# GpSimd's SBUF passes tied to VectorE's 16-bit passes, and other planned times, in a one-core attention block

## The chip, the cores and the metric

The kernel runs on one core of a Trainium2 chip. The metric is the device time of one execution in microseconds; three runs of the kernel before have a median of 369.49 us (368.03 to 369.72).

## The reference

One attention block on x of 1 x 2048 x 448 in bf16, with 16 heads of 28 columns:

```python
qkv = (x @ wqkv).reshape(B, S, 3, H, Dh).transpose(2, 0, 3, 1, 4)
q, k, v = qkv[0], qkv[1], qkv[2]
scores = einsum("bhqd,bhkd->bhqk", q, k) * Dh ** -0.5
p = softmax(scores, axis=-1)
o = einsum("bhqk,bhkd->bhqd", p, v)
return o.transpose(0, 2, 1, 3).reshape(B, S, D) @ wo
```

## The kernel before

The sixteen heads are four groups g of four, and the 2048 queries four chunks c of 512. A set s is one (g, c); there are sixteen, in the order `ORDER`. Each head of a set has sixteen key tiles of 128, so a set is 64 steps of a 128 x 512 block of scores. The heads sit in strips of 32 partitions, 28 of them used; the rows left over carry a bound of the scores, so that the exponentials need no maximum of the row, and a column of ones in V gives the denominators.

A step's exponentials are made in one of two ways. On ScalarE, one activation (line 891, `pt<-a`) takes two steps at once out of a two-bank PSUM tile `a0` or `a1`. On VectorE, a pass over PSUM (line 906, `I<-d`) turns scores into the 16 bits of a bf16 power of two, and two further passes over SBUF (line 929, `J<-I`, 16 bits to 16 bits, up to four steps at once) make shifted copies of them; three weighted copies of V (`VT`, scaled at line 552) bring the three terms together in TensorE's sum `o` (line 987).

The order of the instructions on every engine is written at build time by a planner: a loop at the end of the function keeps a clock for each of TensorE, ScalarE, VectorE, SyncE and GpSimd, takes the engine whose clock is lowest, lets its `pick_` function choose an operation that is ready, and emits it. An operation (`Op`) has a planned duration, the events that it needs and gives, a `lag` that is added to the time at which it is ready, and a `land` that is added to its end before others may use its result (for DMAs). How many steps go each way falls out of this. On the chip the engines run their queues in the emitted order and wait on semaphores for data alone; the planned times are not seen there.

Operations that the planner keeps apart have `port=True`: such an operation of VectorE starts no earlier than the planned end of GpSimd's last one, and the other way round, by the two times in `port`. A J pass reads and sets the same times in `do_add` and `pick_dve`. On GpSimd these are the squares (`square`, line 297, `sq<-KA` and `sq<-QA`), which the norms of keys and queries are summed from, and the products (`mul`, line 1038, `xs<-o_sb,rr` and `OTL<-o_sb,rr`), which divide a set's output. On VectorE they are the J passes, the scaled copies of V, the passes that make `su` and `kmt`, and the reciprocal (line 1025).

When a set is complete, `finish_set` queues this chain: VectorE copies `o` to `o_sb` (line 1016); SyncE's DMA gathers the denominators to `den` (line 1021); VectorE makes the reciprocal `rec`; DMAs write it to `scr` in DRAM (line 1030) and spread it to all rows as `rr` (line 1035); GpSimd multiplies. The output projections (`oproj_job`, and `early_jobs` for the last chunk) need the products of all four groups of a chunk. SyncE's one queue also carries the rows of Q (line 441), the bounds `su` (line 506) and the stores of the output (line 573).

Of the kernel before, what the change touches and what calls it, by code (L numbers as in the profile page):

```python
# [8 lines left out]
ALU = mybir.AluOpType  # L9
AX = mybir.AxisListType  # L10
BF16 = mybir.dt.bfloat16
F32 = mybir.dt.float32
I16 = mybir.dt.int16
# [24 lines left out]
def kernel(  # L38
# [7 lines left out]
    nc = tc.nc  # L46
# [239 lines left out]
    def quarters(out, lhsT, rhs, start, stop, **k):  # L286
        for i in range(P // HP):
            r = slice(HP * i, HP * (i + 1))
            nc.tensor.matmul(out=out[r, :], lhsT=lhsT[:, r], rhs=rhs, start=start, stop=stop, tile_position=(0, HP * i), **k)  # L289

    def new_sq(key):
        sqt[key] = wk.tile([P, QW], BF16, name="sq", tag="sq", bufs=4)
        return sqt[key]

    def square(key, src):
        t = new_sq(key)
        nc.gpsimd.tensor_tensor(out=t[:], in0=src, in1=src, op=ALU.mult)  # L297

    def act_square(key, mask):
        t = new_sq(key)  # L300
# [2 lines left out]
    def k_job(g, sc, bank, pri, gate=0, split=2):  # L303
        key = ("K", g, sc)
        n = CC // split

        def mm(part):
            if part == 0:
                held[key] = bank_tile(bank) if bank[0] != "a" else pair_tile(bank)
            mm_proj(held[key][:, 0:QW], 1, g, sc, range(part * n, (part + 1) * n))  # L310

        def evac():
            KAt[(g, sc)] = big.tile([P, QW], BF16, name=f"KA{sc}", tag=f"KA{sc}", bufs=2)
            src = held[key][:, 0:QW]
            nc.vector.tensor_scalar(out=KAt[(g, sc)][:], in0=src, scalar1=kmask[:, 0:1],  # L315
                                    scalar2=ones[:, 0:1], op0=ALU.mult, op1=ALU.add)

        for p in range(split):
            add("PE", n * D_WAVE, lambda p=p: mm(p), pri=pri, gate=gate, cols=448 * n,
                need=[("XT", sc, 0), ("XT", sc, 1), ("W", 1)] + ([key + (p - 1,)] if p else []), gives=[key + (p,)],  # L320
                acq=bank if p == 0 else None)
        add("DVE", 0.72, evac, need=[key + (split - 1,)], gives=[key], rel=bank, pri=pri)
        add("POOL", 1.15, lambda: square(key, KAt[(g, sc)][:]), need=[key], gives=[("ksq", g, sc)], pri=pri, port=True)

    def kn_job(g, bank, pri, gate=0):
        key = ("KN", g)

        def mm(sc):
            if sc == 0:
                held[key] = bank_tile(bank) if bank[0] != "a" else pair_tile(bank)  # L330
            quarters(held[key][:, 0:QW], maskK[:, sc, :], sqt.pop(("K", g, sc))[:], sc == 0, sc == NQC - 1)

        def red():
            kst[g] = wk.tile([P, 1], F32, name="kst")
            nc.vector.reduce_max(out=kst[g][:], in_=held.pop(key)[:, 0:QW], axis=AX.X)

        def spread_rows():
            a = wk.tile([P, HP], F32, name="kbc")
            nc.vector.tensor_copy(out=a[:], in_=kst[g][:].to_broadcast([P, HP]))
            b = wk.tile([P, HP], F32, name="kbt")  # L340
            nc.vector.transpose(out=b[:], in_=a[:])
            kmt[g] = wk.tile([P, 1], F32, name="kmt")
            nc.vector.reduce_max(out=kmt[g][:], in_=b[:], axis=AX.X)

        for sc in range(NQC):
            add("PE", D_WAVE, lambda sc=sc: mm(sc), pri=pri, gate=gate, cols=512,
                need=[("ksq", g, sc)] + ([("KNp", g, sc - 1)] if sc else []), gives=[("KNp", g, sc)],
                acq=bank if sc == 0 else None)
        add("DVE", 0.61, red, need=[("KNp", g, NQC - 1)], gives=[("kst", g)], rel=bank, pri=pri)
        add("DVE", 0.65, spread_rows, need=[("kst", g)], gives=[("km", g)], pri=pri, port=True)  # L350
# [66 lines left out]
    def q_job(g, c, bank, pri, gate=0, split=2):  # L417
        key = ("Q", g, c)
        n = CC // split
        first = (g, c) == (0, 0)  # L420

        def mm(part):
            if part == 0:
                held[key] = bank_tile(bank) if bank[0] != "a" else pair_tile(bank)
            mm_proj(held[key][:, 0:QW], 0, g, c, range(part * n, (part + 1) * n))

        def evac():
            if first:
                t = qtt[0] = wk.tile([P, QW], BF16, name="qt0", bufs=1)
            else:  # L430
                t = QAt[(g, c)] = big.tile([P, QW], BF16, name=f"QA{c}", tag=f"QA{c}", bufs=1)
            if first:
                nc.vector.tensor_scalar(out=t[:], in0=held[key][:, 0:QW], scalar1=qmask[:, 0:1],
                                        scalar2=qoff[:, 0:1], op0=ALU.mult, op1=ALU.add)
            else:
                nc.vector.tensor_copy(out=t[:], in_=held[key][:, 0:QW])  # L436

        def rows():
            for i in range(HG):
                r = slice(HP * i, HP * i + Dh)  # L440
                nc.sync.dma_start(out=QP[c][i % 2][g % 2][r, :], in_=QAt[(g, c)][r, :])

        for p in range(split):
            add("PE", n * D_WAVE, lambda p=p: mm(p), pri=pri, gate=gate, cols=448 * n,
                need=[("XT", c, 0), ("XT", c, 1), ("W" if g else "G", 0)] + ([key + (p - 1,)] if p else []), gives=[key + (p,)],
                acq=bank if p == 0 else None)
        add("DVE", 0.72 if first else 0.61, evac, need=[("qsq", g, c) if first else key + (split - 1,)], gives=[key], rel=(bank, 2) if first else bank,
            pri=pri)
        if first:
            add("ACT", 0.62, lambda: act_square(key, qmask), need=[key + (split - 1,)], gives=[("qsq", g, c)],  # L450
                rel=(bank, 2), pri=pri)
        else:
            add("POOL", 1.15, lambda: square(key, QAt[(g, c)][:]), need=[key], gives=[("qsq", g, c)], pri=pri, port=True)
            add("SP", 2.4, rows, need=[key, ("QZ", c, g % 2)] + ([("Oset", ORDER.index((g - 2, c)))] if g > 1 else []),
                gives=[("QR", g, c)], land=1.6, pri=1)

# [28 lines left out]
    def qn_job(g, cs, bank, pri, gate=0):  # L485
# [7 lines left out]
        def bound():  # L493
            z = wk.tile([P, QW], BF16, name="z", bufs=1)
            nc.vector.tensor_scalar(out=z[:], in0=held.pop(key)[:], scalar1=kmt[g][:, 0:1], scalar2=MARG4 if g else 1.0,  # L495
                                    op0=ALU.mult, op1=ALU.mult)
            held[("su",) + key] = su = wk.tile([P, QW], BF16, name="su", bufs=1)
            nc.vector.tensor_scalar(out=su[:].bitcast(I16), in0=z[:].bitcast(I16), scalar1=0.5, scalar2=HALFE,
                                    op0=ALU.mult, op1=ALU.add)

        def place():
# [47 lines left out]
    def vs_job(g, b, pri):  # L549
        def scale(k):  # L550
            flat = (lambda v: v.rearrange("p t g e -> p (t g e)")) if g is None else (lambda v: v.rearrange("p t e -> p (t e)"))
            nc.vector.tensor_scalar(out=flat(VT[k][g, b]), in0=flat(VT[0][g, b]), scalar1=WT[k], scalar2=None, op0=ALU.mult)  # L552

        gs = [g] if g is not None else list(range(GH, G))
        for k in range(1, NTERM):
            add("DVE", 0.335 if g is None else 0.2, lambda k=k: scale(k), need=[("V", gs[0], XB * b + u) for u in range(XB)],
                gives=[("VS", gg, b, k) for gg in gs], pri=pri + 0.1 * k, port=True)
# [367 lines left out]
    def do_add(t):  # L925
        ch, m, k = adds[0]
        w = slice(0, m * QW)
        r = ch[k] = wk.tile([P, HG * QW], I16, name=f"J{k}", bufs=NCH)
        nc.vector.tensor_scalar(out=r[:, w], in0=ch["I"][:, w], scalar1=float(SHIFT[k]), scalar2=None, op0=ALU.add)  # L929
        end = port["DVE"] = t + m * QW * 0.00026 + 0.068  # L930
        for n in range(m):
            pending.append({"step": ch["steps"][n], "k": k, "ap": r[:, n * QW:(n + 1) * QW].bitcast(BF16),
# [71 lines left out]
    def finish_set(s, end):  # L1004
# [7 lines left out]
        st = {}  # L1012
# [9 lines left out]

        def recip():
            st["rec"] = wk.tile([P, HG * QW // P], F32, name="rec")
            nc.vector.reciprocal(out=st["rec"][:], in_=st["den"][:])

        def scatter():
            n = P // HG
# [6 lines left out]
            nc.sync.dma_start(out=st["rr"][:], in_=scr[:].unsqueeze(1).to_broadcast([HG, HP, QW]))  # L1035

        def mul():
            nc.gpsimd.tensor_tensor(out=otile(g, c), in0=st["o_sb"][:], in1=st["rr"][:], op=ALU.mult)  # L1038

        add("DVE", 0.61, evac, need=[("Oset", s)], gives=[("osb", s)], rel="o", pri=-5)  # L1040
        add("SP", 0.6, gather, need=[("osb", s)], gives=[("den", s)], land=1.5, pri=2)
        add("DVE", 0.16, recip, need=[("den", s)], gives=[("rec", s)], pri=50, port=True)
        add("SP", 0.35, scatter, need=[("rec", s)], gives=[("scr", s)], land=1.1, pri=2)
        add("SP", 0.5, spread, need=[("scr", s)], gives=[("rr", s)], land=5.5, pri=2)
        add("POOL", 1.4, mul, need=[("rr", s)], gives=[("OT", g, c)], pri=60, port=True)

    def best(eng, t):
        b, nxt = None, None
# [228 lines left out]
```

## Time and profile before

| what | value |
|---|---|
| three runs, median | 369.49 us |
| profiled execution | 368.69 us, span 366.9 us |
| granted clock of TensorE | 1.000 |
| busy: TensorE, VectorE, ScalarE, GpSimd | 345.5, 347.6, 348.9, 70.8 us |
| activations, line 891 | 366 |
| I passes, line 906; J passes, line 929 | 292; 146 |
| squares, line 297; products, line 1038 (GpSimd) | 27; 15 |

The busy times are of the profiled execution. A row of a group has the line, engine, operation, tiles out<-in, shapes and count, then busy time in us and mean ns of one, then the engine's idle time ahead of them with what ended most of it. A row of a timeline has the start and duration in us, the instruction, a count where several are merged, and in brackets the idle time before it with its releaser. A row by tile has the shortest, median and longest duration in ns.

### The profile page before, as it was taken

The page shows a single profiled execution, that of the slowest core. Times are in us where ns is not written, and L with a number is a line of the kernel's source. Part 1 is how long each engine was busy: PE and PEld are TensorE (multiplying, and loading weights), DVE is VectorE, ACT ScalarE, POOL GpSimd, SP SyncE. Part 2 cuts the span into 40 slices and gives each one's busy share as a digit, 9 for nine tenths or more (in the row PEclk, how much of TensorE's full clock was granted, in tenths as well). Part 3 has the DMA queues.
Part 4 walks back from the last instruction along what each step waited for, and adds up shares of the span by engine and source line. Part 5 has one row for each costly group of instructions (what it writes and reads, how often), then busy time and mean ns, then how long its engine had stood idle before and what let it go on. Part 6 is the DMA issues. An engine that isn't in the chain of part 4 may idle for free.

```text
span 366.9 us, 10993 instructions
## 1 busy us (share of the span) xinstructions
PE 345.5 (94%) x4528; PEld 112.3 (31%) x4529; DVE 347.6 (95%) x646; ACT 348.9 (95%) x381; POOL 70.8 (19%) x103
## 2 busy tenths in 40 slices
PE   8999999999999999999889999989988999999985
PEld 4433233422233333232222222222222222222223
DVE  7799999999899999899999999999999999999983
ACT  4689999999999999999999999999999999999992
POOL 8952122123010413121010413201010101010010
PEclk9999999999999999999999999999999999999999
DMA  8510100011000000010000001100000001010101
GB/s 256 123 42 15 28 29 7 4 35 36 18 31 28 6 6 30 15 42 28 15 19 3 30 3 55 31 21 12 19 14 9 26 29 54 19 65 27 46 14 50
DMA packets 15050, 12.30 MB, mean 34 GB/s; under 512 B 6808, under 2 KB 13080, under 8 KB 15000
## 3 DMA queue, kind: packets, MB, share of 16 engines
q1 hardware_dynamic: 13448, 10.18, 9.7%
q10 hardware_dynamic: 1040, 1.02, 0.9%
q8 instruction: 35, 0.57, 0.7%
q0 software_dynamic: 512, 0.40, 0.5%
q14 instruction: 15, 0.12, 0.1%
HBM read 7.58 MB, written 1.96 MB: 26 GB/s over the span
## 4 chain that ended last, share of the span: by engine, by line
PE 34%; ACT 30%; DVE 27%; issue 7%; DMA 1%; DVEq 0%; ACTq 0%
ACT pt L891 30%; DVE I L906 12%; PE a L699 12%; PE o L987 9%; DVE J L929 7%; PE m L289 4%; PE m L282 4%; DVE QP L180 1%; DVE V L540 1%; DVE QA L436 1%; DVE KA L315 1%; DVE z L495 1%; PE d L699 1%; DVE o_sb L1016 1%; DVE V L552 1%
## 5 line engine op out<-in xcount | busy, mean ns | idle before, releaser
L891 ACT ACTIVATE pt<-a 128x1024 bf16<-128x1024 f32 x366 | 337.6, 1145 | 3.0 <-PE a L699 1.4
L906 DVE TENSOR_SCALAR I<-d 128x512 int16<-128x512 f32 x263 | 170.7, 680 | 3.8 <-PE d L699 3.4
L699 PE MATMUL a<-QP,KA 32*128 32x512 bf16 (+1 forms) x720 | 141.0, 381 | 12.2 <-ACT pt L891 11.2
L987 PE MATMUL o<-pt,V 128*32 128x512 bf16 x732 | 104.2, 384 | 0.0
L929 DVE TENSOR_SCALAR J<-I 128x2048 int16<-128x2048 int16 x146 | 101.8, 724 | 0.3
L699 PEld LDWEIGHTS <-KA 32*128 32x128 bf16 (+1 forms) x1041 | 48.7, 91 | 151.2 <-issue 148.3
L699 PE MATMUL d<-QP,KA 32*128 32x512 bf16 (+1 forms) x258 | 83.3, 383 | 1.3 <-DVE I L906 1.3
L987 PE MATMUL o<-J,V 128*32 128x512 bf16 x584 | 76.6, 384 | 0.4 <-DVE J L929 0.3
L987 PE MATMUL o<-I,V 128*32 128x512 bf16 x292 | 68.6, 384 | 0.7 <-DVE o_sb L1016 0.5
L987 PEld LDWEIGHTS <-V 128*32 128x32 bf16 x1608 | 28.6, 94 | 49.6 <-issue 47.0
L1038 POOL TENSOR_TENSOR xs<-o_sb,rr 128x512 bf16<-128x512 f32 x12 | 16.4, 1370 | 105.9 <-DMA rr<-scr 65.0
L282 PE MATMUL m<-XT,WRAW 112*32 112x512 bf16 x384 | 29.6, 384 | 0.2 <-DVE V L540 0.2
L297 POOL TENSOR_TENSOR sq<-KA 128x512 bf16<-128x512 bf16 x12 | 12.5, 1041 | 69.6 <-DVE KA L315 69.6
L297 POOL TENSOR_TENSOR sq<-QA 128x512 bf16<-128x512 bf16 x15 | 16.4, 1091 | 47.4 <-DVE QA L436 47.4
L906 DVE TENSOR_SCALAR I<-m 128x512 int16<-128x512 f32 x29 | 19.7, 680 | 0.4 <-PE m L699 0.4
L289 PE MATMUL m<-WRAW,XT 112*32 112x112 bf16 (+1 forms) x768 | 18.1, 230 | 0.2 <-DVE V L540 0.2
L1038 POOL TENSOR_TENSOR OTL<-o_sb,rr 128x512 bf16<-128x512 f32 x3 | 4.2, 1403 | 56.0 <-DMA rr<-scr 36.7
L289 PEld LDWEIGHTS <-XT 112*32 112x32 bf16 x768 | 11.7, 96 | 10.3 <-issue 10.1
L289 PE MATMUL m<-WO,xs 128*32 128x448 bf16 x156 | 12.5, 359 | 0.0
L436 DVE CAST QA<-m 128x512 bf16<-128x512 f32 x15 | 10.2, 683 | 1.1 <-PE m L282 0.5
L699 PE MATMUL m<-QP,KA 32*128 32x512 bf16 x29 | 11.1, 384 | 0.0
L289 PE MATMUL m<-sq,maskK 128*32 128x512 bf16 x108 | 10.8, 388 | 0.1
(113 smaller groups left out, 192.0 us busy)
## 6 DMA issues: line engine op xcount, KB each, us to landing
rr<-scr SPq DMA_DIRECT2D x15, 256.0 KB
QP<-QA SPq DMA_DIRECT2D x60, 28.0 KB
out_dram<-osb SPq DMA_DIRECT2D x12, 112.0 KB
WRAW<-in_wqkv_dram SPq DMA_DIRECT2D x3, 392.0 KB
xs<-in_x_dram ACTq DMA_DIRECT2D x4, 224.0 KB
xs<-in_x_dram SPq DMA_DIRECT2D x4, 224.0 KB
QP<-su SPq DMA_DIRECT2D x32, 2.0 KB
out_dram<-pt SPq DMA_DIRECT2D x2, 224.0 KB
```

The lines of the kernel that those rows point to most:

```text
L180: nc.vector.memset(QP[c][k][z][:], 0.0)
L282: nc.tensor.matmul(out=ps[HP * i:HP * (i + 1), :], lhsT=w[:, cc, h * Dh:h * Dh + HP], rhs=XT[c][cc // 2][:, cc % 2, :], start=(cc == 0), s ...
L289: nc.tensor.matmul(out=out[r, :], lhsT=lhsT[:, r], rhs=rhs, start=start, stop=stop, tile_position=(0, HP * i), **k)
L297: nc.gpsimd.tensor_tensor(out=t[:], in0=src, in1=src, op=ALU.mult)
L315: nc.vector.tensor_scalar(out=KAt[(g, sc)][:], in0=src, scalar1=kmask[:, 0:1], scalar2=ones[:, 0:1], op0=ALU.mult, op1=ALU.add)
L436: nc.vector.tensor_copy(out=t[:], in_=held[key][:, 0:QW])
L699: nc.tensor.matmul(out=out_ap, lhsT=KAt[(g, j // XB)][r, (j % XB) * P:(j % XB + 1) * P], rhs=q[r, :], start=(n == 0), stop=(n == len(terms ...
L891: nc.scalar.activation(out=pt[:], in_=ps[:], func=ACT.Exp, scale=LN2 / 128.0)
L906: nc.vector.tensor_scalar(out=dst, in0=pd[:], scalar1=BIAS, scalar2=0.0, op0=ALU.add, op1=ALU.max)
L929: nc.vector.tensor_scalar(out=r[:, w], in0=ch["I"][:, w], scalar1=float(SHIFT[k]), scalar2=None, op0=ALU.add)
L987: nc.tensor.matmul(out=o[HP * i:HP * (i + 1), :], lhsT=VT[e["k"]][g, j // XB][:, j % XB, HP * i:HP * (i + 1)], rhs=e["ap"], start=(SETMM[k ...
L1038: nc.gpsimd.tensor_tensor(out=otile(g, c), in0=st["o_sb"][:], in1=st["rr"][:], op=ALU.mult)
```

## The change

`after_shared` gives an instruction a wait on the last VectorE instruction of certain kinds that the planner emitted ahead of it, kept in `cur["shared"]`. The squares of `square` and the products get this wait. Recorded in `cur["shared"]` are the J passes, the scaled copies of V, the pass that makes `su`, the last reduction of `kmt` and the reciprocal. The planned duration of these squares goes from 1.15 to 1.08 and of the products from 1.4 to 1.3; the reciprocal gets a lag of 2.0; the spread of `rr` lands after 7.0 instead of 5.5.

```diff
+    def after_shared(m):
+        if "shared" in cur:
+            tc.add_manual_dep(m.ins, cur["shared"].ins.name,
+                              mybir.DependencyInfo(mybir.DependencyClass.Sync, mybir.DependencyReason.DATA),
+                              reason="GpSimd's pass stays behind VectorE's")
...
     def square(key, src):
         t = new_sq(key)
-        nc.gpsimd.tensor_tensor(out=t[:], in0=src, in1=src, op=ALU.mult)
+        after_shared(nc.gpsimd.tensor_tensor(out=t[:], in0=src, in1=src, op=ALU.mult))
...
-        add("POOL", 1.15, lambda: square(key, KAt[(g, sc)][:]), need=[key], gives=[("ksq", g, sc)], pri=pri, port=True)
+        add("POOL", 1.08, lambda: square(key, KAt[(g, sc)][:]), need=[key], gives=[("ksq", g, sc)], pri=pri, port=True)
...
-            nc.vector.reduce_max(out=kmt[g][:], in_=b[:], axis=AX.X)
+            cur["shared"] = nc.vector.reduce_max(out=kmt[g][:], in_=b[:], axis=AX.X)
...
-            add("POOL", 1.15, lambda: square(key, QAt[(g, c)][:]), need=[key], gives=[("qsq", g, c)], pri=pri, port=True)
+            add("POOL", 1.08, lambda: square(key, QAt[(g, c)][:]), need=[key], gives=[("qsq", g, c)], pri=pri, port=True)
...
-            nc.vector.tensor_scalar(out=su[:].bitcast(I16), in0=z[:].bitcast(I16), scalar1=0.5, scalar2=HALFE,
+            cur["shared"] = nc.vector.tensor_scalar(out=su[:].bitcast(I16), in0=z[:].bitcast(I16), scalar1=0.5, scalar2=HALFE,
...
-            nc.vector.tensor_scalar(out=flat(VT[k][g, b]), in0=flat(VT[0][g, b]), scalar1=WT[k], scalar2=None, op0=ALU.mult)
+            cur["shared"] = nc.vector.tensor_scalar(out=flat(VT[k][g, b]), in0=flat(VT[0][g, b]), scalar1=WT[k], scalar2=None, op0=ALU.mult)
...
-        nc.vector.tensor_scalar(out=r[:, w], in0=ch["I"][:, w], scalar1=float(SHIFT[k]), scalar2=None, op0=ALU.add)
+        cur["shared"] = nc.vector.tensor_scalar(out=r[:, w], in0=ch["I"][:, w], scalar1=float(SHIFT[k]), scalar2=None, op0=ALU.add)
...
-            nc.vector.reciprocal(out=st["rec"][:], in_=st["den"][:])
+            cur["shared"] = nc.vector.reciprocal(out=st["rec"][:], in_=st["den"][:])
...
-            nc.gpsimd.tensor_tensor(out=otile(g, c), in0=st["o_sb"][:], in1=st["rr"][:], op=ALU.mult)
+            m = nc.gpsimd.tensor_tensor(out=otile(g, c), in0=st["o_sb"][:], in1=st["rr"][:], op=ALU.mult)
+            after_shared(m)
...
-        add("DVE", 0.16, recip, need=[("den", s)], gives=[("rec", s)], pri=50, port=True)
+        add("DVE", 0.16, recip, need=[("den", s)], gives=[("rec", s)], pri=50, lag=2.0, port=True)
...
-        add("SP", 0.5, spread, need=[("scr", s)], gives=[("rr", s)], land=5.5, pri=2)
-        add("POOL", 1.4, mul, need=[("rr", s)], gives=[("OT", g, c)], pri=60, port=True)
+        add("SP", 0.5, spread, need=[("scr", s)], gives=[("rr", s)], land=7.0, pri=2)
+        add("POOL", 1.3, mul, need=[("rr", s)], gives=[("OT", g, c)], pri=60, port=True)
```

## The prediction

> **What bounds the kernel now.** I read the page's busy times and costliest groups first, then ScalarE's waits and timeline, then GpSimd's and VectorE's timelines around the same moments.
>
> ```profile
> PE 345.5 (94%) x4528; PEld 112.3 (31%) x4529; DVE 347.6 (95%) x646; ACT 348.9 (95%) x381; POOL 70.8 (19%) x103
> ...
> L891 ACT ACTIVATE pt<-a 128x1024 bf16<-128x1024 f32 x366 | 337.6, 1145 | 3.0 <-PE a L699 1.4
> L906 DVE TENSOR_SCALAR I<-d 128x512 int16<-128x512 f32 x263 | 170.7, 680 | 3.8 <-PE d L699 3.4
> L929 DVE TENSOR_SCALAR J<-I 128x2048 int16<-128x2048 int16 x146 | 101.8, 724 | 0.3
> ```
>
> Three engines are full; GpSimd is idle four fifths of the span. The number of exponentials on ScalarE is fixed by the plan made at build time, so I take ScalarE as the ruler. From its start times in the trace: 366 activations begin at 18.86 us and the last ends at 358.97, 340.1 us; the median distance between two starts is 0.904 us; 366 x 0.904 = 330.9. So 9.1 us are lost between them, 1.0 of it before 26 us, where GpSimd has no pass yet. No removal of waits can give more than about 8 us unless the plan gives ScalarE fewer activations. The timeline of ScalarE has the visible part:
>
> ```profile
> 24.30 73.49 ACT L891 ACTIVATE pt<-a 128x1024 bf16<-128x1024 f32 x80 [0.25 <-PE d L699]
> 98.34 12.50 ACT L891 ACTIVATE pt<-a 128x1024 bf16<-128x1024 f32 x13 [0.55 <-PE a L699]
> 111.05 168.81 ACT L891 ACTIVATE pt<-a 128x1024 bf16<-128x1024 f32 x183 [0.21 <-PE d L699]
> 280.10 73.75 ACT L891 ACTIVATE pt<-a 128x1024 bf16<-128x1024 f32 x80 [0.24 <-PE m L699]
> 354.24 4.72 ACT L891 ACTIVATE pt<-a 128x1024 bf16<-128x1024 f32 x5 [0.40 <-PE a L699]
> ```
>
> The bracket is ScalarE's idle time and who ended it: always TensorE, coming late with scores. What made TensorE late stands in GpSimd's and VectorE's timelines (start, duration, idle before it), and in J's row by tile:
>
> ```profile
> 205.13 1.27 POOL L1038 TENSOR_TENSOR xs<-o_sb,rr 128x512 bf16<-128x512 f32 x1
> ...
> 205.19 1.76 DVE L929 TENSOR_SCALAR J<-I 128x2048 int16<-128x2048 int16 x1
> ...
> 350.18 1.28 POOL L1038 TENSOR_TENSOR xs<-o_sb,rr 128x512 bf16<-128x512 f32 x1 [20.03 <-DMA rr<-scr]
> ...
> 350.38 1.63 DVE L929 TENSOR_SCALAR J<-I 128x2048 int16<-128x2048 int16 x1
> ...
> L929 DVE TENSOR_SCALAR J<-I x146: 627/684/1766, 23.8 to 355.5; 128x2048 int16<-128x2048 int16 x146
> ...
> 96.20 0.25 DVE L1025 RECIPROCAL rec<-den 128x16 f32<-128x16 f32 x1 [1.09 <-DMA den<-o_sb]
> ```
>
> A J pass (median 684 ns) that begins just after a GpSimd pass ends 0.55 us after that pass: it stood still until GpSimd was done. Eight J of the 146 last over 1.1 us, all beside a GpSimd pass, at 39, 54, 107, 205, 231, 250, 288 and 350 us; together 6.1 us over the median. The last line is another loss: VectorE stood 1.09 us at a reciprocal whose denominators had not landed.
>
> **The change, part by part.**
>
> *Wait on VectorE's last shared pass.* The plan never lets a J and a GpSimd pass overlap, but nothing holds GpSimd to it. From the end of a reciprocal the old costs put the product 0.2+0.35+1.1+0.03+0.5+5.5+0.2 = 7.9 us later (8.0 from its start); in nine of fifteen sets it starts 6.5 to 7.2 us after the reciprocal's start. So it comes about a microsecond before its place and lands on a J planned ahead of it: 205, 250, 288, 350. At 39 a square slips between two J that the plan has back to back. The wait stops these. ScalarE's loss behind each, as the distances of its starts over 0.904: 0.26 (39), 0.49 (205), 0.24 (250), 0.39 (288), 0.52 (350), 1.90 in all. At 107 the loss is 0.37 + 0.13 = 0.50, but that product is late (10.2 us after its reciprocal, since the scatter waited in SP's queue behind the su copies), where only the third part below helps; I count half, 0.25. At 54 and 231 the square starts first, right behind its own evacuation, with the J behind it; the wait leaves these as they are: 0.
>
> What the wait costs: behind the waiting instruction on GpSimd stand only the next squares and products. Squares are read by TensorE's norm matmuls; the closest is the square that ends at 90.97 with its matmul at 91.76, 0.79 us of cover, more than one J (0.68). If the cover is gone, TensorE, in order, stands by the rest. Products are needed by the output projections many microseconds later. One more semaphore instruction on GpSimd is 17 ns, on an engine that is 19% busy: 0.
>
> *Squares planned at 1.08 instead of 1.15, products at 1.3 instead of 1.4.* Undisturbed they take 1.04 and 1.27 (the medians by tile). But now the pass starts behind a semaphore: a square behind its evacuation starts 0.14 us after it (QA ends at 80.67, the square starts at 80.81). So the pass ends 0.14 + 1.04 = 1.18 us after the J, where the plan lets the next J go at 1.08: 0.10 late. 21 of the 42 passes end within 0.35 us of the start of a J, so up to 2.1 us of VectorE. In the six collisions above ScalarE lost 2.40 us for 5.02 us of VectorE, 0.48 each: 0 to 1.0 us, and I take 0.5. The shorter costs also free 27 x 0.07 + 15 x 0.1 = 3.4 us of planned exclusion; an activation moved to VectorE costs it two I (2 x 0.6) and half a four-step share of two J (0.6), so at most two activations fewer, 1.8 us. The trace can't show a plan; nearest to zero, since VectorE found I passes to do beside most GpSimd passes. I take 0 and keep -1.8 for the range.
>
> *Reciprocal with a lag of 2.0.* It covers the 1.09 us at 96.2. ScalarE's loss there is one distance of 1.842 instead of 0.904: 0.94 gained. The other fourteen reciprocals had no wait and lose nothing, since nothing on the path waits for them. With the reciprocal its scatter and spread move (issue 0.33 and 0.55 us each on SP): they pass no more than they did, the Q rows and su copies stay in place ahead or behind, and those are needed only a set later.
>
> *Spread with 7.0 instead of 5.5.* The product's place is now 9.5 us from the reciprocal's start, 3.5 later from the gather; thirteen of the fifteen start within 9.5 now. It matters at the end: the product of the last set but one, at 350.18 now, comes at about 353 to 357, beside the last four J, and three early output-projection pieces of 0.19 us each move behind it. TensorE has the 0.24 us before 362.1 free and little else: 0 to 0.6, I take 0.2.
>
> Sum: -1.90 - 0.25 - 0.94 + 0.5 + 0.2 = -2.4 us. The profiled execution took 368.69 us (span 366.9 and 1.8 around it), so 366.3 for such a one; it lies 0.8 below the median of the three runs, 369.49, and the median goes to 367.1.
>
> **The rivals.** *Passes that come late (slower).* The wait holds GpSimd behind VectorE, but nothing holds the next J behind GpSimd. A pass that waits for a late J, or for a landing beyond the new cost (10.2 and 11.1 us occur), runs into the J planned after it, which then stands for up to 1.1 us. For: the 0.10 us handover above, the 21 passes with a J at their end, the SP queue. Against: the spare 1.5 us of the new costs. Price by the collisions above: 0.40 us of ScalarE for each blocked J. With the reciprocal's 0.94 gained, it decides from 11 blocked J instead of 8, and is slower by over 0.5% from 15 of 42; at 17, 9 x 0.40 - 0.94 = +2.7: 372.2 us.
> The Trainium skill (SBUF — State Buffer, section "Who interferes with whom") speaks for this rival: whichever of the two issues first has the shared port pair for its whole instruction, and the other blocks fully. By it a late pass costs a J as before, wait or no wait; the trace agrees at 205.19, where the J ends 0.55 us after GpSimd's pass.
>
> *Nothing measurable.* ScalarE's 8 us stay because most lie elsewhere: 278.66 (0.54), 238.79 (0.29), 102.9 and 104.1 (0.51 together) have no blocked J near them. If the collisions only fill time that would be lost anyway, the reciprocal's 0.94 less the 0.7 of costs remains: 369.2.
>
> *The plan deals better.* Every later decision follows the changed times; with two activations fewer and the stalls gone, -2.4 - 1.8 = -4.2: 365.3. The same dealing can give one or two more, which is in the range above.
>
> That the change doesn't do what it says is hardly possible for the wait; for the costs, a product that starts right behind a J would show it.
>
> **How the numbers follow.** Forecast 0.52, late passes 0.22, better deal 0.14, nothing 0.12. About 0.5% (1.85 us) is what a measurement of this kernel can tell from no change. Of the forecast, with its costs between 0 and 1.6 (a gain of 1.5 to 3.1), four fifths lie beyond that: 0.41 faster, 0.11 same. Faster 0.41 + 0.14 = 0.55; same 0.11 + 0.12 = 0.23; slower 0.22. The forecast's own range is 366.4 to 368.0; for 8 in 10 I go to 364.8 (past the better deal) and to 371.2, which leaves out half of the late passes.
>
> **What would show it.** Right: no J over 1.1 us except behind a square right after its evacuation; J near 690 ns on average; no VectorE wait for den; ScalarE's idle before L891 at 1.5 us or less with 365 to 367 activations; products starting 0.1 to 0.2 us behind a J. Wrong: as many long J as now, behind GpSimd passes that began later; an activation count off by two or more; TensorE waiting for sq; output pieces after 360 us.

## The result and the profile after

The changed kernel takes 366.32 us (median of 6 runs, 366.26 to 366.70) where the kernel before, timed in the same rounds too, has 369.21: 2.89 us less by the medians. The ratio, 0.9927 (95% interval 0.9912 to 0.9942), makes it 2.7 us. The forecast was 2.4 us less than before, 367.1 from a base of 369.49. The profiled execution has a span of 364.6 us against 366.9.

Line numbers are up by 7 or 8 in the changed kernel: activations stand at 898, I at 913, J at 936, the reciprocal at 1032, squares at 304, products at 1045. The page's busy times and groups, with the rows that answer to those shown before:

```profile
PE 346.3 (95%) x4515; PEld 115.5 (32%) x4515; DVE 343.8 (94%) x646; ACT 347.7 (95%) x381; POOL 68.0 (19%) x103
...
L898 ACT ACTIVATE pt<-a 128x1024 bf16<-128x1024 f32 x366 | 336.4, 1186 | 1.7 <-PE d L706 0.8
L913 DVE TENSOR_SCALAR I<-d 128x512 int16<-128x512 f32 x264 | 173.4, 683 | 7.3 <-PE d L706 6.5
L936 DVE TENSOR_SCALAR J<-I 128x2048 int16<-128x2048 int16 x146 | 98.5, 699 | 0.3
```

366 activations, 292 I and 146 J, as before: the plan gave no engine less to do. J costs 98.5 instead of 101.8 us, and VectorE now stands idle ahead of I for 7.3 us instead of 3.8: part of what it saved it only waits away. ScalarE's timeline shows where the time came from:

```profile
24.42 253.65 ACT L898 ACTIVATE pt<-a 128x1024 bf16<-128x1024 f32 x276 [0.25 <-PE d L706]
278.31 78.05 ACT L898 ACTIVATE pt<-a 128x1024 bf16<-128x1024 f32 x85 [0.24 <-PE d L706]
```

The visible holes at 98 (0.55), 111 (0.21) and 354 us (0.40) are gone; the one of 280 stays, now at 278. Counted by start times, what its 366 activations lose over 0.904 us each goes from 9.11 to 6.25 us. J by tile:

```profile
L936 DVE TENSOR_SCALAR J<-I x146: 630/686/1401, 23.9 to 354.0; 128x2048 int16<-128x2048 int16 x146
```

VectorE's and GpSimd's timeline around one product in its new place:

```profile
249.83 0.68 DVE L936 TENSOR_SCALAR J<-I 128x2048 int16<-128x2048 int16 x1
250.43 0.69 DVE L913 TENSOR_SCALAR I<-d 128x512 int16<-128x512 f32 x1
250.59 1.27 POOL L1045 TENSOR_TENSOR xs<-o_sb,rr 128x512 bf16<-128x512 f32 x1 [14.80 <-DVE J L936]
251.03 1.39 DVE L936 TENSOR_SCALAR J<-I 128x2048 int16<-128x2048 int16 x1
```

Whom GpSimd's products wait for (us in total, times, longest):

```profile
POOL xs L1045 <- DVE J L936: 80.1, 7, 18.8
POOL OTL L1045 <- DVE J L936: 57.5, 3, 19.4
```

Ten of the fifteen products are now released by a J; before, eight were released by the landing of `rr` and one by a J. The product at 250.59 starts 0.08 us behind the J that ends at 250.51. Three J over 1.0 us are left (224, 251, 271 us), 1.8 us over the median of before together instead of 6.1. The one at 251.03 still stands behind the product: its place is after the product in the plan, and VectorE had only one I to do in between. No VectorE wait for `den` is left in the list of waits.

### The profile page after: what moved, and what is told of

Same layout as the page of the kernel before. It is cut to its first block, busy times and chain, and to the rows that moved or that the text cites. A ratio compares the mean times of both kernels' runs of the same rounds, so it can differ in the third digit from the quotient of the medians.

```text
span 364.6 us, 10984 instructions
## 1 busy us (share of the span) xinstructions
PE 346.3 (95%) x4515; PEld 115.5 (32%) x4515; DVE 343.8 (94%) x646; ACT 347.7 (95%) x381; POOL 68.0 (19%) x103
## 4 chain that ended last, share of the span: by engine, by line
PE 53%; ACT 32%; issue 7%; DVE 6%; DMA 1%; DVEq 0%; ACTq 0%
ACT pt L898 32%; PE a L706 20%; PE o L994 15%; PE m L282 7%; PE m L289 7%; DVE I L913 2%; DVE J L936 1%; DMA xs<-in_x_dram 1%; PE a L282 1%; PE d L282 1%; DVE QA L443 0%; PE o L738 0%; PE d L289 0%; PE d L706 0%; ACT L146 0%
## 5 line engine op out<-in xcount | busy, mean ns | idle before, releaser
L913 DVE TENSOR_SCALAR I<-d 128x512 int16<-128x512 f32 x264 | 173.4, 683 | 7.3 <-PE d L706 6.5
L994 PE MATMUL o<-pt,V 128*32 128x512 bf16 x732 | 107.2, 384 | 0.1
L936 DVE TENSOR_SCALAR J<-I 128x2048 int16<-128x2048 int16 x146 | 98.5, 699 | 0.3
L706 PEld LDWEIGHTS <-KA 32*128 32x128 bf16 (+1 forms) x1041 | 51.0, 91 | 149.4 <-issue 146.5
L706 PE MATMUL d<-QP,KA 32*128 32x512 bf16 (+1 forms) x259 | 85.7, 384 | 0.0
L994 PE MATMUL o<-J,V 128*32 128x512 bf16 x584 | 79.0, 384 | 0.0
L994 PE MATMUL o<-I,V 128*32 128x512 bf16 x292 | 66.4, 385 | 0.2
L1023 DVE COPY o_sb<-o 128x512 f32<-128x512 f32 x15 | 10.3, 686 | 0.9 <-PE o L994 0.6
L706 PE MATMUL m<-QP,KA 32*128 32x512 bf16 (+1 forms) x28 | 10.8, 384 | 0.0
```

Of the source, the lines that this page charges most:

```text
L706: nc.tensor.matmul(out=out_ap, lhsT=KAt[(g, j // XB)][r, (j % XB) * P:(j % XB + 1) * P], rhs=q[r, :], start=(n == 0), stop=(n == len(terms ...
L913: nc.vector.tensor_scalar(out=dst, in0=pd[:], scalar1=BIAS, scalar2=0.0, op0=ALU.add, op1=ALU.max)
L936: cur["shared"] = nc.vector.tensor_scalar(out=r[:, w], in0=ch["I"][:, w], scalar1=float(SHIFT[k]), scalar2=None, op0=ALU.add)
L994: nc.tensor.matmul(out=o[HP * i:HP * (i + 1), :], lhsT=VT[e["k"]][g, j // XB][:, j % XB, HP * i:HP * (i + 1)], rhs=e["ap"], start=(SETMM[k ...
L1023: nc.vector.tensor_copy(out=st["o_sb"][:], in_=o[:])
```

## The experiments

All but one were timed in five rounds beside the kernel before (`only_J` in three), in three groups, each on another chip. The first group holds the waits alone, the times alone, the lag alone and the shorter lag; the second the waits with the lag, the landing of 5.5, the longer passes in the changed kernel, and `only_J`; the third the rest. The base, the kernel before, had medians of 368.93, 369.56 and 369.12 in them, with single runs 1.8 to 2.7 us apart. "Less than before" is counted against the base of the same group, and ratios have their 95% interval. Two kernels of different groups can be compared in two ways, by their times as they stand or each by its gain over its own base. The two ways differ by up to 0.6 us, and both are given where it matters. A J is called long below when it lasts over 0.8 us, and ScalarE's loss is what its activations lose over 0.904 us each, by start times, after 26 us.

**The waits alone.** The changed kernel with every planned time put back:

```diff
-lag=2.0, ... land=7.0 ... add("POOL", 1.08 ... add("POOL", 1.3
+         ... land=5.5 ... add("POOL", 1.15 ... add("POOL", 1.4
```

> The kernel before with the waits alone: all planned times as before, so the order on every engine is that of before. First theory (passes of GpSimd that start ahead of their planned place block J passes, and the wait stops that): the long J at 39, 205, 250, 288 and 350 us go, three or so stay (54, 107, 231); a gain of 1.4 to 1.9 us against before, some 367.3 to 367.8 where before has 369.2. Second theory (the new planned times deal the work better, and the waits are of no use): within 0.5 us of before. Third (a pass held back runs into the J behind it): as many long J as before or more, and no gain or a loss of up to 2 us.

367.27 us, ratio 0.9956 (0.9939 to 0.9973): 1.66 us less, a gain inside the first theory's range. Its J by tile:

```profile
L936 DVE TENSOR_SCALAR J<-I x146: 628/684/1218, 24.4 to 353.6; 128x2048 int16<-128x2048 int16 x146
```

Its timelines of VectorE and GpSimd at the collision of 205 us, and of VectorE at the remaining wait for `den`:

```profile
205.22 0.69 DVE L936 TENSOR_SCALAR J<-I 128x2048 int16<-128x2048 int16 x1
206.00 1.28 POOL L1045 TENSOR_TENSOR xs<-o_sb,rr 128x512 bf16<-128x512 f32 x1 [0.82 <-DVE J L936]
```

```profile
96.74 0.25 DVE L1032 RECIPROCAL rec<-den 128x16 f32<-128x16 f32 x1 [1.03 <-DMA den<-o_sb]
```

The J that lasted 1.76 us at 205.19 lasts 0.69, and the product that had started 0.06 us ahead of it starts 0.09 us behind it. Of the eight long J one is left, at 54, where the first theory had left three. ScalarE's loss goes from 8.2 to 5.9 us.

**The planned times alone.** The changed kernel, with `after_shared` doing nothing.

```diff
-        if "shared" in cur:
+        if False:
```

> The changed kernel without the waits: its planned times, and so its order on every engine. First theory: the products' data land 2 to 3 us ahead of the planned place, nothing holds GpSimd back, and the long J are as many as before (8) or more; only the reciprocal's wait is gone, 0.9 us: some 368.3. Second theory: as the changed kernel, 366.3, with few long J.

367.47 us, ratio 0.9966 (0.9948 to 0.9985), 1.46 us less than before: neither theory's number. Six J are long, 4.4 us over the median in all, fewer than expected; four of the six stand beside squares (39, 54, 82, 222 us). At 82.40 a square starts while one J runs and gets in ahead of the next; GpSimd's timeline, then VectorE's, where the two J are one row:

```profile
82.40 1.35 POOL L304 TENSOR_TENSOR sq<-QA 128x512 bf16<-128x512 bf16 x1 [2.30 <-DVE QA L443]
```

```profile
82.17 2.13 DVE L936 TENSOR_SCALAR J<-I 128x2048 int16<-128x2048 int16 x2
```

**The lag alone**, in the kernel before:

```diff
-pri=50, port=True)
+pri=50, lag=2.0, port=True)
```

> The kernel before with the reciprocal's lag of 2.0 alone. First theory: VectorE's wait of 1.1 us for den is gone, and with it 0.9 us; six to ten long J stay: some 368.3. Second theory: the later order is dealt anew, anything from 367 to 370, with no tie to the long J.

367.45 us, ratio 0.9961 (0.994 to 0.9981): 1.48 us less, against 0.9 expected. The wait for `den` is gone; the long J are ten, 6.6 us over the median in all, more than the 6.1 of before. So the two causes are separate: this kernel is faster with more VectorE time blocked.

**The waits and the lag together**, landing and durations as before:

```diff
-land=7.0 ... add("POOL", 1.08 ... add("POOL", 1.3
+land=5.5 ... add("POOL", 1.15 ... add("POOL", 1.4
```

> The kernel before with the waits and the lag of 2.0; durations and landing as before. First theory: the two gains add up, 1.66 of the waits alone and 1.4 of the reciprocal (its own loss of 0.88 and the two of 0.28 and 0.24 right behind it, which stayed with the waits alone): 365.9 to 366.5 where before has 369; at most three long J. The longer landing and the shorter passes would then be worth nothing. Rival: the longer landing carries a part (a product planned at 8.0 us behind its reciprocal comes late): 367 or more, with three or more J standing behind late products.

365.84 us, ratio 0.9905 (0.9888 to 0.9923). With this the waits have been put on three different orders of work. The instructions of VectorE, ScalarE and GpSimd come in the same sequence in the two traces of each pair, so that only the waits differ:

| order planned with | without waits, us | with waits, us | waits bring, by the times | by the gains over each base | long J | ScalarE's loss, us |
|---|---|---|---|---|---|---|
| the times of before | 368.93 | 367.27 | 1.66 | 1.66 | 8 to 1 | 8.2 to 5.9 |
| the lag of 2.0 | 367.45 | 365.84 | 1.61 | 2.24 | 10 to 1 | 6.8 to 4.8 |
| all new times | 367.47 | 366.32 | 1.15 | 1.43 | 6 to 3 | 6.4 to 5.3 |

The lag brings 1.48 without the waits and, with them, 1.43 by the times or 2.06 by the gains; ScalarE's loss falls by 1.4 and 1.2 with it. Lag and waits add up within the noise: 1.66 and 1.48 are 3.14, and the two together are 3.72 under their base, with an interval of 2.8 to 4.1. The rest of the change, longer landing and shorter passes, brings nothing: 366.32 and 2.89 under its base with it, 365.84 and 3.72 without.

**A shorter lag.** The changed kernel with 0.4:

```diff
-lag=2.0
+lag=0.4
```

> The changed kernel with a lag of 0.4 instead of 2.0. First theory: VectorE waits about 1 us for den in the set whose gather stands behind the Q rows on SP, and 0.7 to 0.9 us are lost against the changed kernel: 367.0 to 367.2; few long J. Second theory: dealt anew, 365.5 to 368 with no tie to den.

369.73 us, ratio 1.0031 (1.0015 to 1.0048): slower than before, and 3.4 us slower than the changed kernel (3.7 by the gains), where 0.7 to 0.9 was expected. VectorE did wait 0.7 us for `den`, but the large loss is another. TensorE's timeline, then SP's:

```profile
107.61 0.39 PE L706 MATMUL d<-QP,KA 64*128 64x512 bf16 x2 [2.67 <-DMA QP<-su]
```

```profile
99.24 0.48 SPq L1037 DMA_DIRECT2D scr<-rec  x1
101.75 0.61 SPq L1042 DMA_DIRECT2D rr<-scr  x1
102.45 5.42 SPq L513 DMA_DIRECT2D QP<-su  x8
```

The windows view from 106 to 110 us: length, then busy us and instructions of TensorE, its weight loads, VectorE, ScalarE and GpSimd, then granted clock, DMA share and GB/s:

```profile
106.00:110.00 4.00, 2.39 (x19) 0.52 (x19) 1.29 (x2) 1.21 (x2) 1.26 (x1) 0.75 0.03 10
```

With the earlier reciprocal its scatter and spread were planned ahead of the eight `su` copies. The spread waits in SP's queue until the scatter has landed, and the copies that the next set's scores need stand behind it; TensorE is idle for 2.67 us, and its granted clock is 0.75 in that window: 1.00 up to 108 us, 0.52, 0.50 and 0.50 in the three microseconds from there, 0.77 in the next and 1.00 after 112. ScalarE loses 2.9 us in the one distance of its starts that spans the idle time. In the kernel before the copies stand ahead of the scatter, and in the changed kernel too:

```profile
97.78 4.13 SPq L513 DMA_DIRECT2D QP<-su  x8
102.02 0.34 SPq L1037 DMA_DIRECT2D scr<-rec  x1
```

**The spread's landing.** 5.5 in the changed kernel, then 4.5 and 3.0 in the kernel with waits and lag:

```diff
-land=7.0
+land=5.5
...
-land=5.5
+land=4.5     (and 3.0)
```

> The changed kernel with the spread landing after 5.5 again. First theory: most products start 6.5 to 7.2 us behind their reciprocal on the chip, so 8.0 planned is late enough: as the changed kernel within 0.5 us (365.9 to 366.9). Rival: 0.5 to 1.5 us slower than the changed kernel, through products that come late.

> Waits and lag, with the spread planned to land after 4.5: a place 7.0 us behind the reciprocal, so about half of the products come late. By the price of 0.40 us for each blocked J, four to six of them: 367.4 to 368.2. If VectorE has time to spare: 365.6 to 366.8.

> Waits and lag, with the spread planned to land after 3.0: a product's place is 5.5 us behind its reciprocal, where on the chip the earliest came at 6.5. All fifteen products come 1 us or more behind their place and meet the J planned after them. Slower rival of the prediction, at its price of 0.40 us for each blocked J: eight to twelve blocked J more than with 5.5, 3.2 to 4.8 us slower than that kernel's 365.8, 369.0 to 370.6. If a blocked J mostly takes time that VectorE has to spare: 366 to 367.5 with as many long J.

365.93 us (0.9908, 0.989 to 0.9926), 366.00 (0.992, 0.9904 to 0.9936) and 367.91 (0.9961, 0.9945 to 0.9978). With 5.5 in the changed kernel nothing is lost: it is 0.4 us below it by the times, as the first theory had it, and 0.7 by the gains. Against the kernel with waits and lag, whose landing is 5.5, a landing of 4.5 loses 0.2 by the times and 0.6 by the gains, no more than another deal of the plan can move (see below). A landing of 3.0 loses 2.1 by the times or 2.5 by the gains, between the two theories, which had 369.0 to 370.6 and 366 to 367.5.

The count of long J does not set the loss: with 4.5 it goes from one to seven and ScalarE's loss stays at 4.8 us, with 3.0 it goes to ten and the loss to 7.8. The plan with 3.0 has 364 activations instead of 366, and two fewer, 1.8 us of ScalarE, hide a part of that.

GpSimd's timeline and VectorE's at a product that is late against its place, in that kernel:

```profile
143.25 1.27 POOL L1045 TENSOR_TENSOR xs<-o_sb,rr 128x512 bf16<-128x512 f32 x1 [4.53 <-DMA rr<-scr]
```

```profile
143.37 1.70 DVE L936 TENSOR_SCALAR J<-I 128x2048 int16<-128x2048 int16 x1
```

It is released by its data, not by a J, and starts 0.12 us ahead of the J planned behind it. The wait is there and does nothing against this: the mechanism of the slower rival exists, and takes back more than half of the 3.7 us that waits and lag had brought. It is not a pure comparison, since the plan differs too. The Trainium skill (SBUF — State Buffer, section "Who interferes with whom") has the instruction that issues first keep the shared ports to its end; the J ends 0.55 us after the product, as at 205.19 before, so the trace agrees.

**Passes planned for the handover**, first in the changed kernel, then with the landing of before:

```diff
-add("POOL", 1.08 ... add("POOL", 1.3,
+add("POOL", 1.2 ... add("POOL", 1.45,
```

> The changed kernel with squares planned at 1.20 and products at 1.45, so that the 0.14 us of the handover behind a J is planned for. By the prediction's term the changed kernel loses 0.5 us (0 to 1.0) to that handover: 365.3 to 366.3. Rival: the next J is seldom right behind the pass, so that the plan only gets longer exclusions: 366.3 to 367.3.

> Waits and lag with the landing of before, and squares at 1.20 and products at 1.45 as in the kernel that planned for the handover. If the handover is what that kernel gained against the changed one, and the longer landing is worth nothing: 365.0 to 365.7, at or below the best so far. If both gains are of the deal: 365.5 to 366.5.

365.57 us (0.9896, 0.9876 to 0.9915) and 365.36 (0.9899, 0.9883 to 0.9915). By the times both are below their partner, 0.75 under the changed kernel and 0.48 under the kernel with waits and lag; by the gains it is 1.10 and 0.04. So the second pair does not show that the longer passes bring anything. These two are the fastest versions of the study, 0.8 to 1.1 us under the changed kernel in either way of counting.

**What dealing alone moves.** The kernel with waits and lag, with a lag of 2.5:

```diff
-lag=2.0
+lag=2.5
```

> Waits and lag, with a lag of 2.5 instead of 2.0; durations and landing of before. No new effect is in it, only another deal of the plan: how far it lies from the 365.8 of the kernel with 2.0 shows what dealing alone moves. First theory: within 0.6 us. Second theory (dealing is what moves these kernels): 1 us or more off.

366.35 us (0.9927, 0.9912 to 0.9942): 0.5 us above the kernel with 2.0 by the times and 0.95 by the gains, with no new effect in it, and six long J instead of one. So half a microsecond to one is what another deal can do, and differences of that size between plans, those of landing, durations and handover above among them, can't be assigned to one cause.

**Only J, scaled V and `su` recorded.** Reciprocals and the last reduction of `kmt` no longer set `cur["shared"]`:

```diff
-            cur["shared"] = nc.vector.reduce_max(out=kmt[g][:], in_=b[:], axis=AX.X)
+            nc.vector.reduce_max(out=kmt[g][:], in_=b[:], axis=AX.X)
...
-            cur["shared"] = nc.vector.reciprocal(out=st["rec"][:], in_=st["den"][:])
+            nc.vector.reciprocal(out=st["rec"][:], in_=st["den"][:])
```

> The changed kernel, with neither reciprocals nor the last reduction of kmt recorded for the wait: GpSimd then waits for an earlier J, scaled copy of V or su pass. Same order on every engine. If such passes hold nothing of GpSimd's, as the changed kernel within 0.2 us (366.1 to 366.5), and no reciprocal or reduction longer than 0.26 us. If they do, a reciprocal beside a pass lasts over a microsecond and 0.3 to 1 us are lost.

366.59 us (0.9925, 0.9903 to 0.9947), 0.27 above the changed kernel, where at most 0.2 was expected, and by the gains 0.08 better. Its profile has a hole of 0.4 us in ScalarE's starts at 24.5 us, ahead of GpSimd's first new wait (29 us), and ScalarE's loss is no larger than in the changed kernel (5.2 and 5.3). Reciprocals last 243 to 250 ns. They need not be waited for here; whether they would stand behind a pass isn't shown, since the planner keeps them apart.

## Why the prediction was right

- *ScalarE as the ruler, with its count fixed.* Shown: 366 activations before and after, and the loss between them fell by 2.9 us, about the whole gain of 2.7. The two profiled executions differ by 2.3: the first activation starts 0.1 us later, and 0.3 is lost behind the last one.
- *The waits: 1.90 and half of 107, 2.15 in all, less a handover.* Shown in mechanism, by the collision of 205 us alone and by three orders; measured 1.66 on the order of before, where ScalarE's loss fell by 2.2. The working was wrong in two details that cancel by luck. The 0.26 put down to the J at 39 does not come from it: one distance of ScalarE's starts at 40.6 to 41.2 us is 0.25 to 0.28 too long in all fourteen traces, and in eleven of them no J near 39 is blocked. The J at 107 and 231, counted at half (0.25 left out) and at nothing, went too: with the waits alone the product starts at 108.65, behind both J of 107, and the square 0.17 us behind the J of 231. So the plan had these J ahead of the pass. The price of 0.40 us for a blocked J is too high as a mean: over the three orders it is 0.32, 0.23 and 0.36 (2.2, 2.1 and 1.1 us of ScalarE for 7, 9 and 3 J), and it differs from J to J, from nothing at 39 to about 0.5 at 205 and 350.
- *The reciprocal: 0.94.* Mis-sized; the lag brought 1.48 alone, and 1.43 to 2.06 with the waits. The step took one distance of ScalarE's starts alone. With the waits alone that hole stays (0.88), and so do the two right behind it (0.28 and 0.24): together 1.40. The prediction had these two listed under "nothing measurable", as holes with no cause near them. With the lag one of 0.22 is left at 101.5 us; that the two follow from the wait for `den` is argued from their place and from their going with it.
- *The sum.* That it came near is in part luck: the waits brought 0.5 less than the 2.15 put down for them, the lag 0.5 more than its 0.94.
- *Handover, 0.5.* A product starts 0.08 us behind its J, a square mostly 0.17, where the sum took 0.14 for both. Longer planned passes gave 0.75 and 0.48 us by the times, 1.10 and 0.04 by the gains, and dealing moves as much: the cost of 0.5 is not shown.
- *The end, 0.2.* In the trace of the changed kernel twelve matmuls of late output pieces stand ahead of the last projection instead of four, and it starts 0.33 us after the first scaled half is ready (359.45 to 359.78) instead of 0.06 (362.04 to 362.10): 0.27 us. The size is right and the cause is not. The kernel with a lag of 2.5 and the landing of before has the same twelve and 0.33; the one with longer passes and the landing of 7.0 has none and 0.05. So it is the deal, not the landing; and the last product came at 351.08, not at 353 to 357.
- *The reciprocal's DMAs on SP, costed at nothing.* True for the lag of 2.0; the lag of 0.4 shows the price where they stand ahead of the `su` copies, 2.7 us of an idle TensorE. This cover hung on the plan's order and should have stood in the range.
- *Late passes, the slower rival.* The mechanism is real; in the changed kernel too few passes are late for it to decide, and by the lower mean price it needs more blocked J than the 15 given. What a blocked J costs also differs, as the landings of 4.5 and 3.0 show.

## What to carry to other kernels

Two engines that a plan keeps apart must be kept apart by the program too: GpSimd, idle four fifths of the time, ran ahead of its place as soon as its data were there, and its early starts blocked VectorE as late ones do. Price a stall by what the bounding engine loses behind it, over the next several instructions and not the first alone, and look whether that loss goes in a run without the stall. Before two small gains are compared, see that they were measured beside the same base. When a step with DMAs is moved, follow its queue: a transfer that waits in order holds everything behind it.

## What the runs showed that was not expected

How well a kernel repeats goes with the waits, but not with them alone. In the three kernels without them the runs of a group spread over 1.7 to 3.1 us (before 367.87 to 370.59 in the first group and 368.03 to 369.72 beside the changed kernel, the times alone 366.94 to 369.07, the lag alone 366.28 to 369.39). With the waits and a landing of 5.5 or 7.0 behind a lag of 2.0 or more it is 0.2 to 0.8 us (the changed kernel 366.26 to 366.70), and so it is with the waits alone (367.06 to 367.41). With the waits and a landing or a lag planned shorter it is wider again: 1.4 us with the landing of 4.5 (365.67 to 367.06), 2.6 with 3.0 (366.05 to 368.62), and 2.5 with the lag of 0.4 (369.05 to 371.56). The groups have 4 to 21 runs, and a spread grows with their number. I read it as an order that depends on which of two engines comes first, and so differs from run to run; no run tells that directly.
